# Four small loads of x on 2, 6, 8 and 12 partitions behind the third key load of a decode kernel

## The chip, the cores and the metric

The kernel runs on one core of a Trainium2 chip. The metric is the device time of one execution in microseconds. Two runs of the kernel before took 193.44 and 193.47 us, median 193.45. Times inside an execution come from one profiled execution and count from its first instruction; its span, first to last instruction, is 191.2 us.

## What is computed

One token passes an attention over a sliding window, a small MLP branch gates the result, and x is added:

```python
x  = A_x                                   # (1, 1, 512), bf16
xn = _layernorm(x)
s  = _A_ref(xn, k_cache, v_cache, wq, wo)  # attention, below
g  = _silu(_B_ref(xn, w1, w2, w3, w4))
out = x + s * g

def _A_ref(x, k_cache, v_cache, wq, wo):   # 32 heads of 128, window W = 4096
    q = x @ wq                             # one query per head
    k = k_cache[:, :, Sk - W:, :]          # Sk = 32768
    v = v_cache[:, :, Sk - W:, :]
    p = _softmax(q . k * 128 ** -0.5)
    return (p @ v) @ wo                    # wo: (4096, 512)
```

The window of keys is 32 heads x 4096 positions x 128 values in bf16, 33.6 MB, and that of the values the same. With the weights the kernel reads 78.84 MB by the profile.

## The kernel before, in words

**Tiling.** Four heads make a group, so there are eight groups (`NG`). A key or value load of a group brings a tile of 128 partitions x 128 positions x 128 values, 32 KB in each partition, 4 MB together. Partitions 0 to 31 hold the first head of the group, the next 32 the second, and so on. Three key buffers (`K_BUFS`) and two value buffers (`V_BUFS`) rotate.

**Stages.** The loop over `s` from 0 to 9 handles the keys of group s and, two turns later (`LAG` = 2), its values: `h = s - LAG`. Scores of a key tile come in two ways side by side: VectorE multiplies 64 to 80 of the 128 columns by the query (L321) and sums them (L323); for the others TensorE transposes the keys (L339), ScalarE copies them out of PSUM (L342), and TensorE multiplies by the query (L350). Then follow the maximum (L366, L374), the exponentials on ScalarE (L388), and the product with the values on TensorE (L427). For the last group the value load is cut in three parts, and the last part is multiplied at L461. At the end the output projection is summed, gated and added to x (L651, L653), and the output row is stored.

**Order and queues.** `load` (L75 and L76) issues every key, value and weight load on the queue of SyncE (SP) except three: x twice (`x_bf`, `x_row`) and wq go out on ScalarE's queue. SP's loads keep the order of the program. That order is: w2, w3, w4 in two parts, the first key tile in two halves, the second key tile, the third key tile, the first value tile, the fourth key tile, the second value tile, and so on, with wo in three pieces and two loads of `wo_rows` between and behind. PE, VectorE and ScalarE run in the order in which the region writes them by hand.

**Completion semaphores.** Each DMA that SP or ScalarE issues takes the next of eight completion semaphores in turn, and before it goes out it waits for the load that held this semaphore last, that is, for the load eight places ahead of it. It also waits for the readers of the buffer that it fills. The first value tile lies where the weights were, which is why it waits for the work that reads them.

**Memory.** The pools are laid out one behind the other: key buffers, transposed keys, products, constants, `small` (x and other little tiles), the softmax tiles, and then the weights, whose place the value buffers and a part of wo take from turn `s == LAG` on. A tile added to `small` moves all that lies behind it.

Of the kernel before, what the change touches and what calls it, by code (L numbers as in the profile page):

```python
# [9 lines left out]
BF16 = mybir.dt.bfloat16  # L10
# [16 lines left out]
def kernel(  # L27
# [36 lines left out]
    small = ctx.enter_context(tc.tile_pool(name="small", bufs=1))  # L64
# [10 lines left out]
    def load(dst, src):  # L75
        return tc.keep_in_program_order(nc.sync.dma_start(out=dst, in_=src))  # L76
# [18 lines left out]
    def load_kv(pool, cache, g, cuts=(0, CP)):  # L95
        t = pool.tile([P, CP, Dh], BF16, tag="kv", name="kv")
        src = cache[0, G * g:G * g + G, W0:, :].rearrange("a (b c) d -> b a (c d)", b=PB)
        dst = t[:].rearrange("p c d -> p (c d)")
        for c0, c1 in zip(cuts, cuts[1:]):
            load(dst[:, c0 * Dh:c1 * Dh], src[:, :, c0 * Dh:c1 * Dh])  # L100
        return t
# [163 lines left out]
    for i in range(11):  # L265
        n = P if i < 10 else 96
# [44 lines left out]
    def k_open(g):  # L311
        st[g] = {
            "sT": ps_s.tile([P, CP - 64, G], FP32, tag="sT", name="sT"),
            "S": sm_pool.tile([P, CP], FP32, tag="S", name="S"),
        }

    def k_vector(g, kn, part):
        m = nd(g) // 4
        rows = slice(m * part, m * part + m)
        prod = prod_pool.tile([P, 20, Dh], BF16, tag="prod", name="prod")  # L320
        nc.vector.tensor_tensor(out=prod[:, 0:m, :], in0=kn[:, rows, :],  # L321
                                in1=q_bc[:, g:g + 1, :].to_broadcast([P, m, Dh]), op=ALU.mult)
        nc.vector.tensor_reduce(out=st[g]["S"][:, rows], in_=prod[:, 0:m, :], axis=AX.X, op=ALU.add)  # L323
# [3 lines left out]
    def batches(g):  # L327
        n, m = nd(g), CP - nd(g)
        k = -(-m // 8)
        edges = [n + 2 * (m // 2 * i // k) for i in range(k + 1)]  # L330
        return list(zip(edges, edges[1:]))

    def k_turn(g, kn, b):
        c0, c1 = batches(g)[b]
        n = (c1 - c0) // 2
        pt = ps_tr.tile([P, 4, P], FP32, tag="pt", name="pt")
        for i in range(n):
            c = c0 + 2 * i
            nc.tensor.transpose(pt[:, i, :], kn[:, c:c + 2, :].rearrange("p c d -> p (c d)").bitcast(FP32),  # L339
                                ident_f[:])  # L340
        kts[b] = kt_pool.tile([P, 4, 2 * P], BF16, tag="kt", name="kt")
        nc.scalar.copy(out=kts[b][:, 0:n, :], in_=pt[:, 0:n, :].bitcast(BF16))  # L342

    def k_scores(g, b):
        kt = kts.pop(b)
        c0, c1 = batches(g)[b]
        for i in range((c1 - c0) // 2):
            c = c0 + 2 * i - nd(g)
            for l in range(2):
                nc.tensor.matmul(st[g]["sT"][:, c:c + 2, :].rearrange("p c a -> p (c a)"),  # L350
                                 lhsT=kt[:, i, l::2], rhs=q_pair[:, g, l, :], start=(l == 0), stop=(l == 1))
# [55 lines left out]
    def load_wo(i):  # L407
        h0, n = blocks[i]
        load(wo_blk[i], A_wo[h0 * P:(h0 + n) * P, :].rearrange("(p t) n -> p t n", p=P))
# [4 lines left out]
    def load_rows(h, n):  # L414
        load(wo_rows[:, h - h_part:h - h_part + n, :],
             A_wo[h * P:(h + n) * P, :].rearrange("(h p) n -> p h n", p=P))
# [18 lines left out]
    def v_turn(g):  # L435
        s = st[g]
        if g == NG - 1:
            ot_ps = ps_tr.tile([P, 4 * P], FP32, tag="pt", name="ot_ps")
        else:
            ot_ps = ps_misc.tile([P, 4 * P], FP32, tag="misc", name="ot_ps")  # L440
        s["ot"] = ot_ps
        step = P - 4
        for j in range(4):
            nc.tensor.transpose(ot_ps[:, step * j:step * j + P], s["ov_sb"][:, j, :], ident_f[:])  # L444

    def v_add(g):
        s = st[g]
        if g < NG - 1:
            s["oT"] = sm_pool.tile([P, G], FP32, tag="oT", name="oT")
        nc.vector.tensor_reduce(out=s["oT"][:], in_=s["ot"][:].rearrange("p (x m) -> p m x", m=32)[:, 0:G, :],  # L450
                                axis=AX.X, op=ALU.add)
# [58 lines left out]
    def y_open():  # L510
        yr[0] = ps_tr.tile([P, KC, P], FP32, tag="pt", name="yr_ps")
        zeros(yr[0][:])
# [18 lines left out]
    for s in range(NG + LAG):  # L531
        h = s - LAG
        last = h == NG - 1
        kn = load_kv(k_pool, A_k_cache, s, (0, 64, CP) if s == 0 else (0, CP)) if s < NG else None
        if s == LAG:
            wts_guard.__exit__(None, None, None)
            v_pool = ctx.enter_context(tc.tile_pool(name="v", bufs=V_BUFS))
            wo_blk[2] = v_pool.tile([P, 4, D], BF16, tag="wo_4", bufs=1, name="wo_4")
            wo_rows = v_pool.tile([P, H - h_part, D], BF16, tag="wo_rows", bufs=1, name="wo_rows")
        if last:  # L540
            v = load_kv(v_pool, A_v_cache, h, cuts)
            for r in (H - G, H - 2):
                load_rows(r, 2)
        elif h >= 0:
            v = load_kv(v_pool, A_v_cache, h)
        if h == 3:
            wo_24 = k_pool.tile([P, 32, D], BF16, tag="kv", name="wo_24")
            wo_blk[0], wo_blk[1] = wo_24[:, 0:16, :], wo_24[:, 16:24, :]
            load_wo(0)
        if h == 5:  # L550
            load_wo(1)
            load_wo(2)

        if s < NG:
            nb = len(batches(s))

            def keys(b0, b1):
                for b in range(b0, b1):
                    k_turn(s, kn, b)
                    if b > 0:  # L560
                        k_scores(s, b - 1)

            k_open(s)
            k_vector(s, kn, 0)
            keys(0, 2)
            if s == 7:
                v_turn(h - 1)
                v_add(h - 1)
                v_out(h - 1)
            elif s > 1:  # L570
                sm_den(s - 2)
                sm_rden(s - 2)
            elif s == 1:
                sm_max(0)
            k_vector(s, kn, 1)
            keys(2, 4)
            if s == 7:
                sm_den(h)
                sm_rden(h)
                keys(4, nb - 2)  # L580
                sm_turn(s - 1)
                keys(nb - 2, nb)
            else:
                if s > 0:
                    sm_turn(s - 1)
                keys(4, nb)
            k_scores(s, nb - 1)
            sm_own(s)
            if s == 7:
                k_vector(s, kn, 2)  # L590
                v_wide(h, v)
                sm_exp(s - 1)
                v_turn(h)
                y_open()
                k_vector(s, kn, 3)
                v_add(h)
                v_out(h)
                ox_spread(1)
                sm_max(s)
                continue  # L600
            if s > 0:
                sm_exp(s - 1)
            if h > 0:
                v_turn(h - 1)
            k_vector(s, kn, 2)
            if h >= 0:
                v_wide(h, v)
            if h > 0:
                v_add(h - 1)
                v_out(h - 1)  # L610
            if s == 6:
                ox_spread(0)
            k_vector(s, kn, 3)
            if s == 6:
                ox_pick(0)
            if s > 0:
                sm_max(s)
        elif s == NG:
            ox_pick(1)
            sm_turn(NG - 1)  # L620
            sm_exp(NG - 1)
            y_wide(1, False)
            sm_den(NG - 2)
            sm_rden(NG - 2)
            y_wide(0, False)
            warm(3)
            v_wide(h, v)
            sm_den(NG - 1)
            sm_rden(NG - 1)
            v_turn(h)  # L630
            v_add(h)
            v_out(h)
            ox_spread(2)
        else:
            v_open(h)
            warm(3)
            v_wide(h, v, cuts[1], last=False)
            ox_pick(2)
            y_wide(2, True)
            nc.scalar.copy(out=y_sum[:], in_=yr[0][:].rearrange("p j n -> p (j n)"))  # L640
            v_wide(h, v, cuts[2], cuts[1])
            v_turn(h)
            v_add(h)
            rows_add(y_ps, ind, y_sum, False)
            v_part(h, v, cuts[2], CP)
            v_out(h)
            for r in range(H - G, H):
                y_head(r)
# [36 lines left out]
```

## Time and profile before

| | |
|---|---|
| median of two runs | 193.45 us |
| span of the profiled execution | 191.2 us |
| DMA packets, bytes | 4572, 79.02 MB |
| PE busy | 116.4 us, 61% |
| DVE busy | 150.9 us, 79% |
| ACT busy | 89.2 us, 47% |
| POOL busy | 2.3 us, 1% |
| granted TensorE clock, mean | 0.720 |

How to read it: the profile tells of each engine how long its instructions ran, and of DMA which share of the sixteen DMA engines' time was filled with packets. A share is a mean over stages with different limits, so the stages are looked at by themselves. The chain of waits goes back from the last instruction to what released it, step by step, and shows which engine or load was last at each point. Beside the instructions the trace keeps one record for each DMA packet (queue, start, duration, size, but not which of the sixteen DMA engines moved it) and one for each count of a completion semaphore; a large load gives sixteen such counts, one for each DMA engine, and the load is there with the last of them.

### The profile page before, as it was taken

Reading aid. Unit: us, or ns where it says so; the run is one execution under the profiler, and the core shown is the slowest. Engines: PE = TensorE matmul, PEld = TensorE weight load, DVE = VectorE, ACT = ScalarE, POOL = GpSimd, SP = SyncE. Lnnn points to the kernel's source line nnn. Section 1 sums busy time; section 2 is a strip of 40 time slices with the busy share of each in tenths; the row PEclk is TensorE's granted clock in tenths of the full one; section 3 lists DMA queues with packets and bytes.
Section 4 is the critical chain, followed back from the end, with each engine's and each line's share of the span. In section 5 each row is a group of like instructions: output and inputs, shape, how many; then the busy total and the mean of one; then the engine's idle time right before and its main releaser. Section 6 shows DMA issues by size and latency. Waiting matters only on the chain.

```text
span 191.2 us, 2839 instructions
## 1 busy us (share of the span) xinstructions
PE 116.4 (61%) x1159; PEld 74.2 (39%) x1159; DVE 150.9 (79%) x175; ACT 89.2 (47%) x191; POOL 2.3 (1%) x11
## 2 busy tenths in 40 slices
PE   1653754989825368256845772680888189739762
PEld 0430222767614334143334441540763077313322
DVE  1660159979999999999999999999999999980111
ACT  2001370888794076427464564542475148733120
POOL 2110000000000000000000000000000000000000
PEclk9999695555755557955695588557567858975998
DMA  6999999999999999999999999999999998999990
GB/s 211 447 430 404 431 418 439 439 439 437 432 434 439 432 429 432 432 439 432 422 432 432 418 422 418 452 439 435 439 432 434 435 432 372 471 425 405 420 371 32
DMA packets 4572, 79.02 MB, mean 413 GB/s; under 512 B 624, under 2 KB 1232, under 8 KB 1488
## 3 DMA queue, kind: packets, MB, share of 16 engines
q1 hardware_dynamic: 4264, 74.65, 91.6%
q10 hardware_dynamic: 296, 4.20, 5.1%
q8 instruction: 9, 0.15, 0.3%
q14 instruction: 3, 0.02, 0.0%
HBM read 78.84 MB, written 0.00 MB: 412 GB/s over the span
## 4 chain that ended last, share of the span: by engine, by line
DVE 46%; DMA 43%; PE 5%; ACT 3%; issue 1%; SPq 1%; ACTq 0%; DVEq 0%
DMA kv<-in_A_k_cache_dram 31%; DVE S L323 28%; DVE prod L321 15%; DMA kv<-in_A_v_cache_dram 10%; ACT kt L342 3%; DMA x_bf<-in_A_x_dram 2%; PE pt L339 2%; PE ov L427 1%; DVE m L366 1%; DVE S L364 1%; SPq L76 1%; PE sT L350 1%; DVE mx L374 1%; PE oT L461 1%; PE ot_ps L444 0%
## 5 line engine op out<-in xcount | busy, mean ns | idle before, releaser
L323 DVE TENSOR_REDUCE S<-prod 128x20 f32<-128x2560 bf16 (+1 forms) x32 | 86.0, 2686 | 1.1
L342 ACT COPY kt<-pt 128x1024 bf16<-128x1024 bf16 x52 | 51.2, 1013 | 40.4 <-PE pt L339 38.7
L339 PE MATMUL pt<-ident_f,kv 128*128 128x128 f32 x208 | 46.7, 376 | 10.8 <-DMA kv<-in_A_k_cache_dram 10.8
L321 DVE TENSOR_TENSOR prod<-kv,q_bc 128x2560 bf16<-128x2560 bf16 (+1 forms) x32 | 45.4, 1418 | 3.9 <-DMA kv<-in_A_k_cache_dram 3.7
L339 PEld LDWEIGHTS pt<-ident_f,kv 128*128 128x128 f32 x208 | 34.2, 196 | 14.4 <-DMA kv<-in_A_k_cache_dram 10.5
L350 PE MATMUL sT<-q_pair,kt 128*128 128x8 bf16 x416 | 19.4, 170 | 15.7 <-ACT kt L342 15.5
L350 PEld LDWEIGHTS <-kt 128*128 128x128 bf16 x416 | 16.4, 104 | 26.8 <-ACT kt L342 25.8
L427 PE MATMUL ov<-kv,pT 128*16 128x512 bf16 x248 | 22.0, 515 | 1.4 <-DMA kv<-in_A_v_cache_dram 1.4
L388 ACT ACTIVATE pT<-S,mb 128x128 bf16<-128x128 f32 x32 | 13.9, 573 | 0.3
L372 PE MATMUL mt_ps<-ident_f,m 128*1 128x128 f32 x8 | 2.9, 359 | 17.4 <-DVE rden L399 16.9
L433 ACT COPY ov_sb<-ov 128x512 f32<-128x512 f32 x8 | 4.7, 586 | 17.1 <-PE ov L427 17.1
L427 PEld LDWEIGHTS <-pT 128*16 128x16 bf16 x248 | 6.9, 109 | 13.2 <-issue 11.4
L359 ACT ACTIVATE own<-sT,par 128x48 f32<-128x48 f32 (+1 forms) x32 | 7.5, 356 | 3.7 <-PE sT L350 3.7
L444 PE MATMUL ot_ps<-ident_f,ov_sb 128*128 128x128 f32 x32 | 7.1, 359 | 2.9 <-ACT mb L384 1.9
L211 DVE CAST q_row<-qr_ps 128x512 bf16<-128x512 f32 x1 | 0.7, 692 | 9.9 <-PE qr_ps L208 9.9
L388 ACT ACTIVATION_READ_ACCUMULATOR pT<-S,mb 128x1 f32 x32 | 8.3, 258 | 0.0
L372 PEld LDWEIGHTS mt_ps<-ident_f,m 128*1 128x1 f32 x8 | 0.6, 80 | 17.9 <-DVE rden L399 17.2
L399 DVE RECIPROCAL rden<-den_ps 128x4 f32<-128x4 f32 x8 | 1.4, 175 | 7.0 <-PE den_ps L394 7.0
L381 PE MATMUL mb_ps<-md,par_t 5*128 5x4 f32 x16 | 3.9, 311 | 4.1 <-DVE md L376 4.1
L255 ACT ACTIVATE a_row<-a_ps 128x384 bf16<-128x384 f32 x1 | 0.5, 491 | 12.0 <-remote 12.0
L444 PEld LDWEIGHTS ot_ps<-ident_f,ov_sb 128*128 128x128 f32 x32 | 4.5, 178 | 3.9 <-ACT mb L384 2.3
L208 PE MATMUL qr_ps<-wq_sb,xq_bf 128*1 128x512 bf16 x32 | 3.1, 566 | 3.7 <-DMA wq_sb<-in_A_wq_dram 3.7
(122 smaller groups left out, 81.6 us busy)
## 6 DMA issues: line engine op xcount, KB each, us to landing
kv<-in_A_k_cache_dram SPq DMA_DIRECT2D x7, 4096.0 KB, 31.3
kv<-in_A_v_cache_dram SPq DMA_DIRECT2D x7, 4096.0 KB, 30.6
wq_sb<-in_A_wq_dram ACTq DMA_DIRECT2D x1, 4096.0 KB, 17.6
kv<-in_A_k_cache_dram SPq DMA_DIRECT2D x2, 2048.0 KB, 27.4
wo<-in_A_wo_dram SPq DMA_DIRECT2D x1, 2048.0 KB
kv<-in_A_v_cache_dram SPq DMA_DIRECT2D x1, 2048.0 KB
kv<-in_A_v_cache_dram SPq DMA_DIRECT2D x2, 1024.0 KB, 17.6
w_sb<-in_B_w_dram SPq DMA_DIRECT2D x1, 1376.0 KB, 9.1
```

What stands on the lines that cost most here:

```text
L321: nc.vector.tensor_tensor(out=prod[:, 0:m, :], in0=kn[:, rows, :], in1=q_bc[:, g:g + 1, :].to_broadcast([P, m, Dh]), op=ALU.mult)
L323: nc.vector.tensor_reduce(out=st[g]["S"][:, rows], in_=prod[:, 0:m, :], axis=AX.X, op=ALU.add)
L339: nc.tensor.transpose(pt[:, i, :], kn[:, c:c + 2, :].rearrange("p c d -> p (c d)").bitcast(FP32), ident_f[:])
L342: nc.scalar.copy(out=kts[b][:, 0:n, :], in_=pt[:, 0:n, :].bitcast(BF16))
L350: nc.tensor.matmul(st[g]["sT"][:, c:c + 2, :].rearrange("p c a -> p (c a)"), lhsT=kt[:, i, l::2], rhs=q_pair[:, g, l, :], start=(l == 0), ...
L359: nc.scalar.mul(s["own"][:, 0:m, a], s["sT"][:, 0:m, a], par[:, a:a + 1])
L372: nc.tensor.transpose(mt_ps[:], s["m1"][:], ident_f[:])
L381: nc.tensor.matmul(mb_ps[:], lhsT=par_t[:].rearrange("k b a -> k (b a)"), rhs=md[:], start=True, stop=True)
L388: nc.scalar.activation(out=s["pT"][:, :, a], in_=s["S"][:], func=ACT.Exp, scale=scale, bias=mb[:, a:a + 1], accum_out=s["sum"][:, a:a + 1])
L427: nc.tensor.matmul(ov[r:r + 4 * G], lhsT=s["pT"][:, c:c + 4, :].rearrange("p i a -> p (i a)"), rhs=v[:, c:c + 4, :], start=(i < 4), stop=( ...
L433: nc.scalar.copy(out=s["ov_sb"][:], in_=ov[:])
L444: nc.tensor.transpose(ot_ps[:, step * j:step * j + P], s["ov_sb"][:, j, :], ident_f[:])
```

## The change

At turn `s == LAG`, after the third key load is issued and before the weights' pool is given up and the first value load is issued, a tile `few` of 16 partitions x 4 x 16 is taken from `small`. Four loads fill parts of it from the start of x: 2, 6, 8 and 12 rows of 16 values, 32 bytes each. They go out by `load`, on SP's queue. Nothing reads `few`.

```diff
         kn = load_kv(k_pool, A_k_cache, s, (0, 64, CP) if s == 0 else (0, CP)) if s < NG else None
         if s == LAG:
+            few = small.tile([16, 4, 16], BF16, name="few")
+            for i, k in enumerate((2, 6, 8, 12)):
+                load(few[0:k, i, :], A_x[0, 0, 0:16 * k].rearrange("(k n) -> k n", k=k))
             wts_guard.__exit__(None, None, None)
             v_pool = ctx.enter_context(tc.tile_pool(name="v", bufs=V_BUFS))
```

## The prediction

> **What bounds the kernel now.** I read the slices and queue totals of the page first, because a kernel that loads 79 MB may simply be waiting for its loads.
>
> ```profile
> span 191.2 us, 2839 instructions
> ...
> DMA  6999999999999999999999999999999998999990
> GB/s 211 447 430 404 431 418 439 439 439 437 432 434 439 432 429 432 432 439 432 422 432 432 418 422 418 452 439 435 439 432 434 435 432 372 471 425 405 420 371 32
> DMA packets 4572, 79.02 MB, mean 413 GB/s; under 512 B 624, under 2 KB 1232, under 8 KB 1488
> ...
> q1 hardware_dynamic: 4264, 74.65, 91.6%
> q10 hardware_dynamic: 296, 4.20, 5.1%
> ```
>
> The reader is to see that the DMA engines are busy in every slice but the first and the last two or three, at a rate that hardly moves (most slices 418 to 439 GB/s). q1 is the queue of SP, on which the change adds its loads. The same in stretches, with the last three columns clock, DMA share and GB/s:
>
> ```profile
> 20.00:31.00 11.00, 6.82 (x70) 2.63 (x67) 5.65 (x6) 5.15 (x10) 0.00 (x0) 0.81 1.03 432
> 31.00:52.00 21.00, 17.61 (x175) 14.13 (x171) 19.73 (x16) 15.29 (x20) 0.00 (x0) 0.55 1.02 437
> 52.00:72.00 20.00, 9.64 (x95) 7.19 (x98) 19.73 (x15) 12.03 (x32) 0.00 (x0) 0.53 1.00 430
> 72.00:130.00 58.00, 35.59 (x359) 22.37 (x351) 57.35 (x44) 30.29 (x75) 0.00 (x0) 0.69 1.00 432
> ...
> 168.00:184.00 16.00, 10.68 (x101) 4.37 (x104) 4.59 (x17) 3.90 (x17) 0.00 (x0) 0.79 0.99 421
> 184.00:191.00 7.00, 2.87 (x68) 1.64 (x67) 0.98 (x4) 0.75 (x2) 0.00 (x0) 0.91 0.35 133
> ```
>
> The third busy column is DVE: it is full too from 31 to 130 us, but falls to 4.59 of 16.00 at the end, where DMA is still at 0.99. So DMA sets the end. Next the chain of waits (start, us, what), for what the last stretch hangs on:
>
> ```profile
> 5.29 36.53 DMA kv<-in_A_k_cache_dram
> ...
> 130.25 23.26 DMA kv<-in_A_k_cache_dram
> ...
> 167.79 18.54 DMA kv<-in_A_v_cache_dram
> 186.33 0.05 issue
> 186.38 0.97 PE oT L461 x32
> ```
>
> The chain runs through DVE between 41.9 and 130 us, yet it ends in loads. What follows the last landing, 186.33 us, is 4.9 us. Last, when SP issues (start, us):
>
> ```profile
> 2.59 4.77 SPq L76 DMA_DIRECT2D kv<-in_A_k_cache_dram  x4
> 31.19 0.53 SPq L76 DMA_DIRECT2D kv<-in_A_v_cache_dram  x1
> 41.85 0.53 SPq L76 DMA_DIRECT2D kv<-in_A_k_cache_dram  x1
> 42.44 0.60 SPq L76 DMA_DIRECT2D kv<-in_A_v_cache_dram  x1
> ```
>
> The third key load is issued by 7.36 us; SP then only waits until 31.19. By the trace's semaphore records that key load lands, engine by engine, from 49.88 to 51.63 us. Loads stand 20 us and more ahead in the queue, so SP may be late by that much and DMA still has work.
>
> **The change part by part.** It removes nothing. The program's order puts the four loads between the third key load and the first value load, as the diff says.
>
> *Waits of SP.* Each DMA takes the next of eight completion semaphores and waits for the DMA that last held it. The four loads so wait in turn for the wq load (19.87 us by the semaphore records), for w3 (10.32), for the first part of w4 (20.89) and for its second part (21.23). Four issues follow; SP's other issues take 0.39 to 0.66 us each in this profile, and the one load on 4 partitions, x_row on ACT, took 1.11. At 1.11 each the last is issued at 21.23 + 1.11 = 22.3 if the earlier ones went out in their waits, and at 19.87 + 4 x 1.11 = 24.3 if not. Queued behind them is the value load, which waits for DVE and PE until 31.19: price 0, with 6.9 us of cover. If that cover were gone, the value load's place in the queue, after 49.88 us, would hide another 18.7 us.
>
> *Semaphores handed on.* All later loads move four semaphores on. The new conditions that are not just renamed: the second value load waits for the second key load (landed 41.82, the value load went out at 42.44), the fifth key load for the third (51.63 against 57.38), the third value load for the first (61.29 against 73.95), the sixth key load for a tiny one (before 57 against 75.55). After that everyone waits for the load eight places ahead, as before. The smallest margin is 0.6 us, and behind it stand 28 us of queue (the load moves from 70 us on). Price 0.
>
> *DMA work.* This is the only term on the path. 2 + 6 + 8 + 12 = 28 rows of 32 bytes, one packet each, and one 4-byte semaphore packet for each engine of each load. In the packet records of before, packets of 4 and 8 bytes take 9 ns, those of 256 bytes 15 to 18. x_row, 4 partitions, landed in four counts (6.17, 6.19, 6.28, 6.81) after one record for the other twelve: one row to each of four engines. So if rows go to engines one by one from the same end, the fullest engine gets 4 data and 4 semaphore packets: 4 x (18 + 9) = 0.11 us, at least 4 x (9 + 9) = 0.07. In the records the next load's first packet starts 6 ns behind a semaphore packet (25.030, then 25.036), so joints add some 4 x 0.012 = 0.05. Together 0.12 to 0.16 us on an engine, and the end moves by that only if this engine is also the last.
>
> The Trainium skill, "DMA: Bandwidth & Descriptors", section "Why a DMA increments its semaphore by 16 and not by 1", says that such a load uses the largest number of engines up to 16 that divides its rows, the lowest-numbered ones; two engines would then bear all four loads. The counts of x_row agree for four; which engines they are no run here shows.
>
> Which engine is last? Engines do not end together: the last value load lands from 184.31 to 186.33. The spread grows with the nine 16 KB instruction packets (queue 8, 0.96 to 1.10 us each), each of which sets one engine back by some 1.3 to 1.9 us. As nine engines at most are set back, I take half: +0.06 us, ends 0 and +0.16.
>
> *Layout.* The new tile puts 128 bytes into the pool `small`, so the softmax tiles, the weights and the value buffers move up by 128 bytes; the key buffers stay. Key and value rows, at different offsets today, both take 1.213 us per 32 KB packet, so DMA gives no sign of caring. PE's read of values (L427, 515 ns mean) could change, but PE has 10.68 of 16 us busy where the end is made, and what it does after the last landing is 0.97 us. Bounds: a tenth of that, 0.1 us, either way; I take 0.
>
> Sum: 191.2 + 0.06 = 191.3 us of span. The median of the runs, 193.45, stands 2.25 above the profiled span; added, 193.5 us.
>
> **The rivals.**
>
> *A: each tiny load empties its rings, and the time is slower.* An engine would not start the next packet of the queue until the tiny one has landed. The price is the time of a lone small load: the output store, 1 KB, issued at 188.68 and landed at 190.35, so 1.67 us; four in a row 6.7 us on the fullest engine, 200.2 us in all. It decides once a load costs over 0.97 us (3.87 / 4). x_bf, 4.0 us to landing, would make it 16 us. For: 32 bytes are far below any row that now stands in q1 (its smallest data packet there before the output is 1 KB), and a load's end is that of its slowest engine, so one engine is enough. Against: semaphore packets of large loads are followed in 6 ns, and with 1 KB packets the stretch from 20 to 31 us shows no hole (DMA share 1.03). Chance 0.09. The Trainium skill, same page, section "Rules for kernel authors", speaks against the change: transfers under 64 KB pay mostly overhead. Its fit of 2.0 us fixed per DMA (section "Anatomy of one DMA", for another issue path) would give an estimated 8 us if the fixed parts added up; the key loads that land 9.7 us apart at 432 GB/s show that they overlap here for large loads.
>
> *B: the spread of the engines changes for the worse.* If two instruction packets came to fall on one engine, or PE fetched at other moments, the last engine would be one step of 1.3 to 1.9 us later: 194.8 to 195.4. For: nine fetches in the trace, and nothing that I know holds them apart. Against: PE's instructions are the same in number and order. Chance 0.07; still within 2%.
>
> *C: the spread changes for the better*, or the layout helps PE at the end: at best the last engine comes to the middle, half of 2.0 us, so 192.5. Chance 0.03.
>
> *D: SP's waits bite.* They would have to exceed 20 us; the semaphores that they wait for land by 21.23. With everything unnamed that costs more than 2%: 0.02. More than 2% faster would need 189.6; engine time is at its floor (each 32 KB packet takes 1.213 us, 16 times 27.0 GB/s), and only 2 us of idle start, 2 us of spread and 4.9 us after the last landing are left: 0.02. That the loads are not made, or elsewhere, the order of the program excludes.
>
> **How the numbers follow.** No change to speak of (193.3 to 193.8): 0.77; A 0.09; B 0.07; C 0.03; D 0.02; faster 0.02. Two percent, 3.87 us, is about what a measurement of this kernel can tell from no change. Within it lie the first case, B and C: 0.87; slower A and D: 0.11; faster 0.02. The range takes the first case and most of B: 193.0 to 195.2, and leaves out A, D, the gain and the better half of C, some 0.15.
>
> **What would show it.** Right: a packet count in q1 higher by 28 data packets and 2 + 6 + 8 + 12 semaphore packets, four tiny issues on SP between 19.9 and 24.5, the first value load still at 31.2, the third key load's last landing at 51.6, DMA share 1.00 from 52 to 72 us, the last value landing near 186.4. A would show as engine idle time near 50 us and all later landings later by the same amount. B would show as a last value load whose engines land over more than 2.0 us. I am wrong if DMA is full throughout and the time still moves by over 1 us: then packets themselves take longer than 1.213 us, for which I have no mechanism.

## The result, and the profile after

The changed kernel took 194.57 us (two runs, 194.56 and 194.59) against 193.45: 1.12 us or 0.56% more, ratio 1.0056 with a 95% interval from 1.0037 to 1.0075. That is slower, inside the range and within 2%, but 0.8 us above the upper end of the case that was called likeliest. One run of those below (the tile without its loads, 199.19 us) fell in a slower state of the chip and is left out.

The page of the changed kernel, the rows that answer to those of before:

```profile
span 192.3 us, 2841 instructions
...
DMA  6999999999999999999999999999999999999990
GB/s 178 445 460 392 427 419 443 436 436 434 430 431 429 436 419 436 429 436 436 419 436 429 422 419 409 450 436 433 436 429 431 426 436 388 477 419 392 416 357 18
DMA packets 4628, 79.02 MB, mean 411 GB/s; under 512 B 680, under 2 KB 1288, under 8 KB 1544
...
q1 hardware_dynamic: 4320, 74.65, 91.4%
```

The span is 1.1 us longer. There are 56 more packets, all of them on SP's queue and under 512 bytes: 28 rows and 28 semaphore writes. DMA is as full as it was. So DMA did not wait; it moved the same 79.02 MB more slowly. Two of the stretches shown for before (the last columns are clock, DMA share, GB/s):

```profile
72.00:130.00 58.00, 36.80 (x363) 22.90 (x355) 57.35 (x44) 30.07 (x75) 0.00 (x0) 0.68 1.00 429
...
168.00:184.00 16.00, 11.09 (x101) 4.72 (x102) 5.25 (x17) 4.12 (x18) 0.00 (x0) 0.79 0.98 414
```

The share is 1.00 and 0.98 as before (1.00 and 0.99), but the rates are 429 and 414 GB/s in place of 432 and 421. The shorter stretches of the prediction go either way (20 to 31 us: 438 in place of 432; 31 to 52 us: 425 in place of 437; 52 to 72 us: 435 in place of 430), as this execution began 0.3 us late and a packet counts whole where it starts. So the rates alone decide nothing; the packets below do. SP's issues (start, us) show no wait that would explain it:

```profile
20.11 1.66 SPq L76 DMA_DIRECT2D few<-in_A_x_dram  x4
31.50 0.55 SPq L76 DMA_DIRECT2D kv<-in_A_v_cache_dram  x1
42.28 0.53 SPq L76 DMA_DIRECT2D kv<-in_A_k_cache_dram  x1
42.85 0.61 SPq L76 DMA_DIRECT2D kv<-in_A_v_cache_dram  x1
57.80 0.54 SPq L76 DMA_DIRECT2D kv<-in_A_k_cache_dram  x1
```

The four loads go out while SP would have waited. What follows is 0.3 to 0.4 us later than before, and so is the first half of the first key tile, which was in the queue ahead of them (landed at 26.30, before 25.99): this execution began slower. A second profile of the same kernel (below) began 0.06 us late in place of 0.3, so this part is scatter. The end of the chain of waits (start, us, what):

```profile
168.44 18.80 DMA kv<-in_A_v_cache_dram
187.25 0.05 issue
187.29 0.97 PE oT L461 x32
```

The last value load lands at 187.25, 0.92 us later than before (186.33), and the output lands 0.92 later too (191.27 and 190.35). From the output's landing to the end of the span it is 1.08 us, and was 0.83. So of the longer span 0.92 us arise ahead of the last landing and 0.25 behind the output's landing, and they have different causes.

The 0.25 first. At the end of the program SP waits for the completion semaphores one after the other. Its wait for the output store before and after, from the list of SP's waits (us in total, times, longest), is longer after, because SP comes to it earlier:

```profile
SPq L680 <- DMA out_dram<-out_row: 0.7, 1, 0.7
```

```profile
SPq L683 <- DMA out_dram<-out_row: 1.0, 1, 1.0
```

The store takes 1.67 us from issue to landing in both. The trace has the six steps of the wait: they take the semaphores in the same order in both kernels, and follow each other by about 0.06 us. Before, the store held the semaphore of the last step, and the other five were over while it was under way; the last one starts at 190.37 us, with the landing. Four loads more move the store four semaphores on, to the one of the second step. That step now starts with the landing, at 191.29 us, and the four others follow behind it, the last at 191.53. These four steps are the 0.25 us.

Now the 0.92. From the packet records I worked out when the kernel had moved a given number of bytes, and subtracted the same time of the kernel before. The third key load ends and the tiny loads come between 19.5 and 21 MB. This is no view of the profile, but a table made from the trace (us):

```text
                        19.5 MB  21 MB  40 MB  60 MB  78 MB
changed kernel            0.32    0.35   0.47   0.59   0.82
the same, second profile  0.06    0.06   0.18   0.29   0.53
```

At the tiny loads it lost 0.00 to 0.03 us. Behind them it lost 0.47 us, evenly. The reason is in the packets: a 32 KB packet of a value load took 1213.0 ns before and 1216.8 after (mean of four loads, without those beside an instruction packet). Three to four ns in 1213 are 0.3%.

### The profile page after: what moved, and what is told of

The parts are those of the page before. It is cut to its first block, busy times and chain, and to the rows that moved or that the text cites. A ratio compares the mean times of both kernels' runs of the same rounds, so it can differ in the third digit from the quotient of the medians.

```text
span 192.3 us, 2841 instructions
## 1 busy us (share of the span) xinstructions
PE 117.6 (61%) x1159; PEld 74.2 (39%) x1159; DVE 150.9 (78%) x175; ACT 89.1 (46%) x191; POOL 2.3 (1%) x11
## 2 busy tenths in 40 slices
DMA packets 4628, 79.02 MB, mean 411 GB/s; under 512 B 680, under 2 KB 1288, under 8 KB 1544
## 4 chain that ended last, share of the span: by engine, by line
DVE 46%; DMA 43%; PE 5%; ACT 2%; issue 1%; SPq 1%; ACTq 0%; DVEq 0%
DMA kv<-in_A_k_cache_dram 31%; DVE S L323 28%; DVE prod L321 15%; DMA kv<-in_A_v_cache_dram 10%; DMA x_bf<-in_A_x_dram 2%; PE pt L339 2%; ACT kt L342 2%; PE ov L427 1%; PE sT L350 1%; DVE m L366 1%; SPq L76 1%; DVE S L364 1%; DVE mx L374 1%; PE oT L461 1%; PE ot_ps L444 0%
## 5 line engine op out<-in xcount | busy, mean ns | idle before, releaser
L339 PE MATMUL pt<-ident_f,kv 128*128 128x128 f32 x208 | 45.9, 371 | 10.5 <-DMA kv<-in_A_k_cache_dram 10.5
L339 PEld LDWEIGHTS pt<-ident_f,kv 128*128 128x128 f32 x208 | 33.7, 194 | 14.2 <-DMA kv<-in_A_k_cache_dram 10.0
L427 PE MATMUL ov<-kv,pT 128*16 128x512 bf16 x248 | 22.8, 530 | 1.5 <-DMA kv<-in_A_v_cache_dram 1.4
L381 PEld LDWEIGHTS mb_ps<-md,par_t 5*128 5x128 f32 x16 | 3.6, 275 | 5.5 <-PE sT L350 4.1
```

The lines of the kernel that those rows point to most:

```text
L381: nc.tensor.matmul(mb_ps[:], lhsT=par_t[:].rearrange("k b a -> k (b a)"), rhs=md[:], start=True, stop=True)
L427: nc.tensor.matmul(ov[r:r + 4 * G], lhsT=s["pT"][:, c:c + 4, :].rearrange("p i a -> p (i a)"), rhs=v[:, c:c + 4, :], start=(i < 4), stop=( ...
```

## The experiments

Two theories: the *layout* costs (L, later split into V for value buffers and S for softmax tiles), or the *loads* cost (D). Ratios are to the kernel before on the same chip. The lines shown from the profiles are windows of one stretch, 54 to 118 us, in which only keys, values and no weights or wo are loaded; the last two columns are DMA share and GB/s. The kernel before and the changed kernel, one fence each:

```profile
54.00:118.00 64.00, 36.52 (x369) 24.07 (x369) 63.21 (x48) 34.77 (x81) 0.00 (x0) 0.66 1.01 433
```

```profile
54.00:118.00 64.00, 37.09 (x369) 24.39 (x369) 63.21 (x48) 34.63 (x81) 0.00 (x0) 0.65 1.00 429
```

DVE (third busy column) does the same work to the hundredth, and DMA moves 429 GB/s in place of 433. The view is coarse, as a packet counts where it starts: runs whose value packets took 1213.0 ns show 431 to 433 here. The packets tell more, so the table at the end of this section has them.

**The tile without its loads.**

```diff
             few = small.tile([16, 4, 16], BF16, name="few")
-            for i, k in enumerate((2, 6, 8, 12)):
-                load(few[0:k, i, :], A_x[0, 0, 0:16 * k].rearrange("(k n) -> k n", k=k))
```

> The tile few is taken at the same place, its four loads are left out: only the move of the softmax tiles, weights and value buffers by 128 bytes is left. Theory L (the layout costs, because 32 KB packets of loads take 1.216 to 1.218 us instead of 1.213 once the value buffers no longer stand on a multiple of 256 bytes): 194.4 to 194.6 us, ratio to before about 1.0055, and value packets of 1.217 us. Theory D (the four loads cost, by queue time or by shifting the DMA engines against each other): 193.45 us, ratio 1.000, value packets of 1.213 us. If both share it, about 194.0.

Measured: 194.24 us, ratio 1.0042 (1.0029 to 1.0055). Most of the change's cost, with no load in it. In its profile the stretch runs at 428 GB/s:

```profile
54.00:118.00 64.00, 36.92 (x369) 24.32 (x369) 63.21 (x48) 34.51 (x80) 0.00 (x0) 0.66 1.00 428
```

**The loads, with the old layout.**

```diff
-    small.tile([P, 96], BF16, name="pad")
+    small.tile([P, 32], BF16, name="pad")
```

> The four loads stay, and the pad at the head of the pool small is made 128 bytes shorter, so that the softmax tiles, weights and value buffers lie where they lay before (x and the query copy move down by 128 bytes instead). Theory L: 193.4 to 193.6 us, ratio 1.000. Theory D: 194.4 to 194.6 us, ratio about 1.0055.

Measured: 193.81 us, ratio 1.0024 (1.0014 to 1.0035). Neither theory: the loads alone cost 0.44 us, more than the 0.06 of the prediction, less than D. Of this, 0.25 us are the four steps behind the output's landing, which the profile of this run shows too (1.08 us from the output's landing to the end). This leaves some 0.2 us for the queue. The rate of the stretch is back:

```profile
54.00:118.00 64.00, 36.81 (x369) 24.50 (x369) 63.21 (x48) 34.85 (x81) 0.00 (x0) 0.63 1.00 432
```

The profile is that of the longest of the twelve runs (194.43 us), and most of what it has above the median lies behind the last value landing: PE, at a granted clock of 0.53 from 160 to 180 us (0.83 in the profile of before), was late with its work, and the last multiply began 0.8 us after the last landing and not at once. So this profile is read for packets and semaphores only.

**The loads, and a step of 256 bytes.**

```diff
-            few = small.tile([16, 4, 16], BF16, name="few")
+            few = small.tile([16, 8, 16], BF16, name="few")
```

> The four loads stay, and the tile few is twice as long (256 bytes), so that all behind it moves by 256 bytes and the value buffers stand on a multiple of 256 again, though at another address. Theory L with the step of 256: 193.4 to 193.6 us, ratio 1.000, value packets of 1.213 us. Theory L with any move at all, or theory D: 194.4 to 194.6 us.

Measured: 193.79 us, ratio 1.0028 (1.0018 to 1.0039), value packets of 1213.0 ns. The same as with the old layout, so it is not the move that slows packets, but where the buffers come to stand.

**The changed kernel again, on that chip.**

> The changed kernel once more, on the same chip as its parts. Both theories: 194.57 us, ratio 1.0056. If its time came from the chip or from the one program's start and not from the change, the ratio would fall within 0.999 to 1.001.

Measured: 194.33 us, ratio 1.0046 (1.0034 to 1.0058). The change is real. The tile (1.0042) and the loads (1.0024) add to 1.0066, above this; with these intervals it is not shown whether they add up or not. The packet records point to less than the sum: near the tiny loads the kernels with four loads and value buffers on a multiple of 256 lost 0.11 to 0.28 us, the changed kernel 0.00 to 0.03 (first table at the end of this section).

**Only the value pool moved.**

```diff
             v_pool = ctx.enter_context(tc.tile_pool(name="v", bufs=V_BUFS))
+            v_pool.tile([P, 64], BF16, bufs=1, name="v_pad")
```

> The kernel before, with 128 bytes taken at the head of the value pool: value buffers and two small blocks of wo move by 128 bytes, weights and softmax tiles stay, no tiny loads. Theory V (it is the place of the value buffers that makes load packets slow, 1.217 us in place of 1.213): the time to have moved 78 MB grows by about 0.47 us against 21 MB, and the kernel takes 0.5 to 0.9 us more, ratio 1.003 to 1.005. Theory S (it is the softmax tiles or the weights): packets of 1.213 us, ratio 1.000.

Measured: 194.08 us, ratio 1.0031 (1.0020 to 1.0041), 0.47 us lost between 21 and 78 MB, as in the changed kernel. V holds; the rate of the stretch is down as well:

```profile
54.00:118.00 64.00, 37.90 (x370) 25.02 (x369) 63.21 (x48) 34.40 (x80) 0.00 (x0) 0.63 1.00 430
```

**Softmax tiles moved by 128 bytes, value buffers by 256, no loads.**

```diff
+            few = small.tile([16, 4, 16], BF16, name="few")
+            sm_pool.tile([P, 64], BF16, bufs=1, name="sm_pad")
             wts_guard.__exit__(None, None, None)
```

> The tile few without loads, and 128 bytes more in the softmax pool: softmax tiles move by 128 bytes (those allocated later by 256), weights and value buffers by 256, so that they stand on a multiple of 256 again. Theory V: value packets of 1.213 us, ratio 1.000. Theory S: packets of 1.217 us, ratio 1.004.

Measured: 193.40 us, ratio 0.9998 (0.9986 to 1.0010), and the stretch runs at the old rate. S falls.

```profile
54.00:118.00 64.00, 37.70 (x369) 24.98 (x369) 63.21 (x48) 34.95 (x81) 0.00 (x0) 0.63 1.01 433
```

**Sixteen rows in each load, old layout.**

```diff
-            for i, k in enumerate((2, 6, 8, 12)):
+            for i, k in enumerate((16, 16, 16, 16)):
```

> As the kernel with the four loads and the old layout (ratio 1.0024), but with 16 rows in each of the four loads in place of 2, 6, 8 and 12, so that every DMA engine gets the same. Theory U (the uneven counts set the engines against each other, and that costs): ratio 1.000 to 1.001. Theory T (each tiny load holds up the engine that meets it, however many meet it): ratio 1.002 to 1.004.

Measured: 193.80 us, ratio 1.0022 (1.0011 to 1.0034). With equal counts it costs as much as with uneven ones (1.0024), as T said. But 0.25 us of both, 0.13%, are the steps behind the output's landing, which neither theory had. With them added U would have said 1.0013 to 1.0023, and 1.0022 fits this as well as T. So whether the uneven 2, 6, 8 and 12 cost anything is not shown. In the semaphore records the slowest engine counts the third key tile at 51.29 and then the four loads at 51.46, 51.62, 51.79 and 51.95: 0.16 to 0.17 us each.

**Four loads behind each key load, 24 in all.**

```diff
             few = small.tile([16, 24, 16], BF16, name="few")
...
+        if LAG < s < NG:
+            for i, k in enumerate((2, 6, 8, 12)):
+                load(few[0:k, 4 * h + i, :], A_x[0, 0, 0:16 * k].rearrange("(k n) -> k n", k=k))
```

> The four loads six times over, behind each key load from the third to the eighth, 24 loads in all, with the value buffers on a multiple of 256 as before. Theory T (some 0.2 to 0.4 us of queue time for each group of four): 1.2 to 2.4 us more than before, ratio 1.006 to 1.013. Theory P (a tiny packet costs its 9 ns and a joint of 6, 0.12 us for a group, and the rest of the 0.4 us that the one group cost is a shift of the engines that is paid once): 0.7 to 1.1 us more, ratio 1.004 to 1.006. SP is held longer by the waits of the later groups; if that starved the queue, DMA idle time would show behind 50 us.

Measured: 194.95 us, ratio 1.0088 (1.0062 to 1.0114), so 1.5 us for six groups, inside T. But the profile has only 1.06 us of this ahead of the last value landing, 0.18 for each group: the upper end of P and less than T. Another 0.21 us pass between this landing and the output's, and 0.29 between the output's landing and the end, where SP's last but one step comes 0.4 us later than before (why is not shown). So T and P are not told apart. The price is not the same for each group, either. By bytes moved two groups (near 69 and 89 us) lost 0.25 and 0.28 us and the other four 0.05 or nothing. SP's issues show what else the loads do:

```profile
42.45 10.06 SPq L76 DMA_DIRECT2D few<-in_A_x_dram  x4
52.55 0.54 SPq L76 DMA_DIRECT2D kv<-in_A_v_cache_dram  x1
57.38 0.54 SPq L76 DMA_DIRECT2D kv<-in_A_k_cache_dram  x1
61.23 10.93 SPq L76 DMA_DIRECT2D few<-in_A_x_dram  x4
```

The second group waits ten microseconds for a key load eight places ahead, and the value load behind it goes out at 52.55 in place of 42.44. It still stood in the queue long before its turn near 71 us, so no queue ran dry. The idle time that DMA shows near 69 us (0.94 of 16 engines over 2 us) lies where the second group's packets are.

**Key buffers on a multiple of 256 too.**

```diff
+    k_off = ctx.enter_context(tc.tile_pool(name="k_off", bufs=1))
+    k_off.tile([P, 64], BF16, name="k_off")
     k_pool = ctx.enter_context(tc.tile_pool(name="k", bufs=K_BUFS))
...
-    small.tile([P, 96], BF16, name="pad")
+    small.tile([P, 32], BF16, name="pad")
```

> The kernel before, with 128 bytes ahead of the key pool and 128 fewer in the pad of small: key buffers too stand on a multiple of 256, value buffers and weights lie where they lay. Theory V: the second and third key tile (1217.5 ns a packet before) come down to 1213 ns, 32 packets of each DMA engine at most 4 ns faster, so 0.07 to 0.15 us less; ratio 0.999 to 1.000. Theory E (only buffers that stand at the same offset disturb each other): value and key buffers now share one, packets of 1217 ns, ratio 1.003 to 1.004.

Measured: 193.26 us, ratio 0.9995 (0.9986 to 1.0004). Packets of keys and values took 1213.0 ns throughout. E falls. This is the best layout in the records, but its time can't be told from the kernel before. Its profile, that of the longest of its eleven runs (193.84), shows why earlier loads need not help: the last value load landed at 185.75 us, 0.58 earlier than before, but PE, at a granted clock of 0.57 from 183 to 186 us (1.00 before), began the last multiply 0.87 us after this landing.

**The offsets the other way round.** As above, without the change of the pad.

> The offsets the other way round: key buffers on a multiple of 256, value buffers and weights 128 bytes behind one. Theory V in its narrow form (value buffers alone matter): ratio 1.003 to 1.004 and packets of 1217 ns. Theory W (a load into a buffer on a multiple of 256 brings the engines into step and the next load, at 128, still gains; it needs one aligned stream in two): ratio 0.999 to 1.001, packets of 1213 to 1214 ns once the second key load runs. Theory E gives the same as W.

Measured: 193.56 us, ratio 1.0012 (1.0003 to 1.0020), key packets 1213.0, value packets 1213.3. With keys on a multiple of 256, value buffers at 128 cost little: W holds for the packets, the narrow V falls; that W's reason is the true one, engines brought into step, is not shown. The stretch runs at 431 GB/s, between the two.

**Value buffers 64 bytes behind a multiple of 256.**

```diff
+            v_pool.tile([P, 32], BF16, bufs=1, name="v_pad")
```

> The kernel before with 64 bytes at the head of the value pool in place of 128: value buffers 64 bytes behind a multiple of 256. Theory V (anything but a multiple of 256 is slow): packets of 1217 ns or more, ratio 1.003 or more. If a multiple of 64 is enough: 1213 ns, ratio 1.000.

Measured: 194.14 us, ratio 1.0045 (1.0033 to 1.0058), packets of 1217.0 ns. A multiple of 64 is not enough, and 64 bytes cost as much as 128.

**The 24 loads with value buffers at 128.** The kernel with four loads behind each key load, and the value pool moved by 128 bytes as above.

> The 24 tiny loads of the run before (ratio 1.0088 with value buffers on a multiple of 256), and value buffers 128 bytes behind it. Theory A (the price of the loads and that of the place add up): 1.0088 + 0.0031, so 1.011 to 1.013, 195.6 to 196.0 us. Theory H (in the slow layout the engines have the tiny rows read by the time that they come to them, so that these cost only their 9 ns and joints, as in the changed kernel's records): 1.003 to 1.007, 194.0 to 194.8 us, and no DMA idle time behind the groups.

Measured: 195.06 us, ratio 1.0085 (1.0071 to 1.0099). Neither theory: with 24 loads the place of the value buffers adds nothing that can be told (1.0088 without it), although packets are slower (1216.0), and DMA idle time behind a group is there, near 69 us. H falls, and A too. In the two profiles the offset does cost something: from 21 to 78 MB the kernel lost 0.79 us, and 0.54 with the same loads and the values at 0, so the offset costs 0.25 us there and not 0.47, and the last value load landed 0.35 us later (187.74 and 187.39).

The packets of all layouts, worked out from the trace; offsets are those of the buffers behind a multiple of 256 bytes, durations are means in ns of the loads between 52 and 117 us, and the last two columns are what the kernel lost against the one before (us) from 19.5 to 21 MB, where the first tiny loads are, and from 21 to 78 MB:

```text
                          keys at  values at  value pkt  key pkt  19.5-21  21-78
before                      128        0       1213.0    1213.8     -        -
changed                     128      128       1216.8    1217.3    0.03     0.47
changed, second profile     128      128       1217.1    1217.6    0.00     0.47
tile without loads          128      128       1217.2    1217.4   -0.01     0.48
only value pool moved       128      128       1216.8    1217.5    0.00     0.47
value pool moved by 64      128       64       1217.0    1217.5   -0.01     0.48
loads, old layout           128        0       1213.0    1213.6    0.17    -0.03
loads, step of 256          128        0       1213.0    1213.3    0.28    -0.06
loads of 16 rows            128        0       1213.0    1213.4    0.11    -0.03
softmax tiles moved         128        0       1213.0    1214.0    0.04     0.00
keys at 0, values at 128      0      128       1213.3    1213.0   -0.06     0.00
both at 0                     0        0       1213.0    1213.0   -0.03    -0.13
```

And the end of some of these profiles, from the trace (us), with the place of the store's semaphore among SP's six steps:

```text
                          last value  to output's  to the  store's
                          load lands  landing      end     step
before                      186.33      4.02        0.83    last
tile without loads          187.02      4.02        0.84    last
only value pool moved       186.95      4.26        0.83    last
both at 0                   185.75      5.11        0.83    last
changed                     187.25      4.02        1.08    second
changed, second profile     186.84      4.02        1.08    second
loads, old layout           186.43      4.77        1.08    second
loads, step of 256          186.53      4.02        1.08    second
loads of 16 rows            186.32      4.29        1.08    second
24 loads                    187.39      4.23        1.12    last
```

With four more loads the time from the output's landing to the end is 1.08 us in every profile, without loads 0.83 or 0.84.

## Why the prediction was right, and where it was wrong

*DMA sets the end*: right for the kernel before and the changed one. The delay of the last landing, 0.92 us, is the delay of the output, and from the one to the other it took 4.02 us in both. It is no rule of this kernel: in the profiles of the loads with the old layout and of both pools at 0, PE was late and the last multiply began 0.8 to 0.9 us after the last landing.

*SP's waits, price 0*: right. The four loads went out from 20.11 us and the value load at 31.50.

*Semaphores handed on, price 0*: right for the loads, and wrong at the end of the program. The closest new wait (second value load, 42.85, for the second key load, landed 42.23) had 0.6 us to spare, as said. But the step stopped there: "After that everyone waits for the load eight places ahead, as before." The output store was handed on as well, from the last step of SP's closing waits to the second, and this costs 0.25 us on the path.

*DMA work, 0.06 us, ends 0 and 0.16*: about right for the changed kernel. The rows came as 28 data and 28 semaphore packets, by 2, 6, 8 and 12 counts. The Trainium skill, "DMA: Bandwidth & Descriptors", section "Why a DMA increments its semaphore by 16 and not by 1", says that only the engines which such a load uses add to its semaphore; the trace agrees. In the changed kernel's own records the rows follow each other by 12 ns, as worked out, and cost 0.03 us. With value buffers on a multiple of 256 the same four loads cost 0.17 and 0.28 us of queue time. The joint of 6 ns was read from large loads; between tiny ones it can be longer: with the old layout four of the 28 rows start 0.06 to 0.25 us behind every other small packet. Why is not shown.

*Layout, taken at 0 with 0.1 us either way*: this step failed, and it holds the largest share, 0.47 us. The sentence "Key and value rows, at different offsets today, both take 1.213 us per 32 KB packet, so DMA gives no sign of caring" is true of the median over all 32 KB packets of SP's queue. By load the records of before already told them apart: the second and third key tile, ahead of any value load, took 1217.5 ns a packet, every value load 1213.0. Moving the value pool alone costs 0.31% (0.20 to 0.41). The bound was put on PE's reads, which are not where the time went.

The parts add up. In the second profile of the changed kernel the span is 0.76 us longer than before: 0.06 of late start, 0.00 at the tiny loads, 0.48 of slower packets and 0.25 behind the output's landing make 0.79. In the first one 0.92 at the last landing, 0.32 of them a late start, and 0.25 behind the output's landing make the 1.17 by which its span is longer.

*Rival A, a tiny load empties its rings for 1.67 us*: did not come. The semaphore counts of tiny loads on one engine lie 0.16 to 0.24 us apart, and the deciding point was 0.97. *B and C, the spread of the engines*: 2.02 us at the last value load before, 2.04 after; neither came. *The median*: the 2.25 us around the span held (194.57 less 192.3 is 2.27).

The range held by luck: B's price, kept in it for another reason, covered the 1.1 us. The prediction had named its own sign of being wrong, "if DMA is full throughout and the time still moves by over 1 us: then packets themselves take longer than 1.213 us, for which I have no mechanism", and longer packets came, though they are only 0.47 of the 1.1 us.

Four things stay open. Why an offset makes packets slower is not shown. It is no fixed price of the address: before, key buffers at 128 got 1217.5 ns ahead of the value loads, but 1213.8 between value loads that stand at 0; and in two runs with the same offsets (loads of 16 rows, softmax tiles moved) the second key tile, also ahead of the value loads, took 1213.3. The Trainium skill, "DMA: Bandwidth & Descriptors", section "How a descriptor splits into AXI transactions", says that a descriptor which does not start on a multiple of 256 bytes also fetches the bytes from the boundary to its start. By the rate here (32,768 bytes in 1213 ns) 128 bytes are an estimated 4.7 ns, near the measured 3.8. The trace agrees in size for 128, but not for 64 bytes, which cost the same, nor for the keys between aligned values; and the sources did not move. Why a group of tiny loads costs 0 at one time and 0.28 us at another is open too, and so is whether their price in the queue and that of the offset add up: for 24 loads the medians show no sum (1.0085 with both, 1.0088 without the offset), the two profiles about half of what the offset costs alone. And the medians of the three kernels that have only the offset, without loads, stand 0.64 to 0.87 us above the kernel before, more than the 0.47 or 0.48 that their packets account for; where the rest goes is not shown.

## What to carry to other kernels

In a kernel that DMA bounds, a term of 0.3% on every packet outweighs a visible but single cost: look at where each large buffer starts before looking at what a small new tile does. When two streams stand at different offsets, compare their packets load by load and not by one median. A tiny load that nobody waits for, in a full queue, is worth tenths of a microsecond for four, not microseconds. When loads are added, follow the completion semaphores to the very end of the program: which one the last store gets decides how many waits come behind it.

## What the runs showed of the hardware that was not expected

Load packets of 32 KB took 1213.0 ns in every load when all large buffers stood on a multiple of 256 bytes in their partition, and 1216.8 to 1217.6 when keys stood at 128 and values at 64 or 128 (1216.0 with 24 tiny loads between them); one aligned stream of two was nearly enough (1213.0 and 1213.3). Key loads at 128 took 1217.5 ns ahead of the value loads and 1213.8 between value loads on a multiple of 256. Semaphore counts of tiny loads on one DMA engine came 0.16 to 0.24 us apart, even where their packets were 12 ns apart. SP's closing waits took 0.06 us a step, and four of them fell behind the output's landing because the store held another semaphore, 0.25 us in all. With a granted clock of 0.57 in place of 1.00 near the end, PE and not the last load set the end of one profile.
